# Reordering the front of a fused attention and mixer kernel: k casts, zero products, first pair and gathered rows, one relu

## The chip, the cores and the metric

The kernel runs on one core of a Trainium2 chip. The core has five engines, each with its own in-order instruction queue: TensorE (PE in the profile, with its weight loads PEld), VectorE (DVE), ScalarE (ACT), GpSimd (POOL) and SyncE (SP, which issues DMAs here). They meet only through semaphores. The metric is the time of one launch on the device, in microseconds (us); lower is better.

## The reference

Attention over 8 batches, 8 heads, 576 positions and 64 dimensions, in which a row sees its neighbours within 32 positions, and 8 global positions see all and are seen by all. What it gives is turned into `[batch, 576, 512]` and goes through a mixer: one two-layer product over positions, one over channels, each with a residual.

```python
scores = q @ k^T / 8;  mask = |i - j| <= 32 or global[i] or global[j]
x  = softmax(where(mask, scores, -1e9)) @ v            # heads side by side: [B, 576, 512]
u  = x + (relu(x^T @ w_tok1) @ w_tok2)^T               # 576 -> 256 -> 576
out = u + relu(u @ w_ch1) @ w_ch2                      # 512 -> 1536 -> 512
```

Inputs and output are float32; the kernel computes its products in float16 with float32 sums.

## The kernel before

Heads go in four pairs (`p`), rows in five tiles of 128 (`t`, `tau`), of which the last holds 64. For one batch the steps are:

- **casts** (`cast_qk`, L364, and L361 for the last 64 rows): q and k from float32 (`lq`, `lk`, `lr`) to float16 (`qk`, `rn`). q, k and v of batch 0 come in by DMAs on SP at the start; those of batch 1 by SP as well, once the casts have freed the buffers.
- **transposes**: `T` (L432) turns the four q and four k tiles of a pair on TensorE into a PSUM tile `pT`; `TE_q` and `TE_k` (L436, L442) copy it out in row order into `qT` and `kT`. `TR` (L454 to L456) does so for the last rows. From batch 3 on DMA transposes and the copies `order_k`, `order_q` take their place.
- **scores** (`S_`, L467): a band of scores per pair in two PSUM tiles, then exponentials on ScalarE (L487, L504, L509) into `e_all`. In batch 0 the mask is added on TensorE, as products of `far` with the identity (L475); `far` is built by `masks_r` and `masks_l` on VectorE out of `pcol`, five column products (L299). From batch 1 on `SM` multiplies the exponentials by `bandm` on VectorE (L531) and copies the global columns to `eg` (L525); in batch 0 it only copies (L521).
- **global rows**: `gather` (L205, four indirect DMAs on GpSimd for each half of the batches) fetches the q and k rows of the global positions by row numbers (`idx_i`, made in `row_numbers`); `gather_t` casts them on VectorE (L337), transposes them on TensorE (L338, tile `pg`) and copies them to `gT` and `kgz`. Batch 0 gets its own by products with a one-hot matrix (`G0`, L416). `GK` makes their scores, `OG` (L553) their part of the output, `PV` (L574 to L591) the weighted sum of v and the division.
- **mixer over positions**: `M1` (L606), a relu, `M2` (L630, L636, L639; for batch 0 also `M23_first` and `M3_first`, L647 to L663), giving `u`, and its transpose `uT` (by DMA from batch 1 on).
- **mixer over channels**: `M4`, twelve products `b1p` of four matmuls (L683) with a relu each: on ScalarE (L689), for odd ones of batch 0 on VectorE (L687); `M4l` for the last rows of two batches; `M5` (L712), `op`, in halves of six matmuls, with the residual added on VectorE (L716) and a store on SP.

The order is written out by hand; no scheduler moves anything, and each engine takes its instructions in the order of the program. The front of batch 0 stands at the end of the function. Then `period(b)` runs for each batch: it lists the channel products of batch `b` in `dense` (twelve M4, then M5 in halves), and `d(k)` takes the next `k` of them between the attention steps of batch `n = b + 1`. `scores(p, k)` is the attention step of one pair, `keep` holds some dense steps back for later, and `tail` says how many go early. PSUM has three double-bank buffers (`psS`, by `pss`) for scores, transposes, `pg`, `pv`, `hp` and `pcol`, and two single banks (`psM`, by `psm`) for `b1p` and `op`; `misc` and `idle` hold the latter two at first. A tile that takes a buffer waits for the last reader of the one before. Six products of zeros (L866) into `idle` stand at the very front; nothing reads them.

Of the kernel before, what the change touches and what calls it, by code (L numbers as in the profile page):

```python
# [26 lines left out]
def kernel(  # L27
# [32 lines left out]
    def pss(shape, dtype=F32, name="s"):  # L60
        return psS.tile(shape, dtype, tag="s", name=name)
# [211 lines left out]

    misc = psm([P, 512], name="misc")
    idle = psm([P, 512], name="idle")
    pcol = pss([P, 2, 512], name="pcol").rearrange("p a b -> p (a b)")

    def masks_0():
        gidx_h = const.tile([1, NG], F16)
# [15 lines left out]
        return isgb  # L295

    def column_products(isgb):
        for t in range(NT):
            nc.tensor.matmul(pcol[:, P * t : P * t + P], lhsT=isgb[:, t, :], rhs=ident, start=True, stop=True)  # L299

# [9 lines left out]

    def masks_r(c):
        nc.vector.scalar_tensor_tensor(
            out=far[:, c, 80:208], in0=pcol[:, P * c : P * c + P], scalar=rowok[:, c : c + 1], in1=right, op0=ALU.add,
            op1=ALU.add,
        )

    def masks_l(c):
        nc.vector.scalar_tensor_tensor(
            out=far[:, c, 0:64], in0=pcol[:, P * c - 64 : P * c], scalar=rowok[:, c : c + 1], in1=left, op0=ALU.add,
            op1=ALU.add,  # L320
        )

# [4 lines left out]
    def masks_c():  # L327
# [2 lines left out]
        nc.gpsimd.tensor_copy(out=it_f, in_=it_i)  # L330
        nc.gpsimd.tensor_scalar(out=mf, in0=it_f, scalar1=gpm, scalar2=hi8, op0=ALU.is_equal, op1=ALU.add)

    def gather_t(t):
        copy = nc.vector.tensor_copy
        pg = pss([P, 2, P], F16, name=f"pg_{t}")
        for ti in range(2):
            copy(out=g16[ti][t], in_=g32[ti][t])  # L337
            nc.tensor.transpose(out=pg[:, ti, :], in_=g16[ti][t], identity=ident)  # L338
        b0 = 1 if t == 0 else 0
        bs = slice(4 * t + b0, 4 * t + 4)  # L340
        pk = pg.rearrange("p i (b n g) -> p i b n g", b=4, n=NP)[:, :, b0:]
        copy(out=gT[:, bs], in_=pk[:, 0])
        for par in range(2):
            r = slice(64 * par, 64 * par + 64)
            copy(out=kgz[r, bs, :, GW * par + NG : GW * par + GW], in_=pk[r, 1])
# [50 lines left out]
    def order(b, p):  # L396
        order_k(b, p)
        order_q(b, p)
# [42 lines left out]
    def TE_k(b, p, copy):  # L441
        copy(  # L442
            out=kTs[b % 2][:, p, WIN : WIN + 512].rearrange("p (x i) -> p x i", i=4),
            in_=st[b]["pT", p][:, 1].rearrange("p (i x) -> p x i", i=4),
        )

    def TE(b, p, copy):
        TE_q(b, p, copy)
        TE_k(b, p, copy)

    def TR(b, copy):
        pr = pss([P, NP, P], F16, name=f"pr_{b}")
        for p in range(NP):
            nc.tensor.transpose(out=pr[:, p], in_=rn[:, p], identity=ident)  # L454
        copy(out=qTs[b % 2][:, :, NT - 1, GW : GW + LAST], in_=pr[:, :, 0:LAST])
        copy(out=kTs[b % 2][:, :, WIN + 512 : WIN + S], in_=pr[:, :, LAST:P])  # L456
# [208 lines left out]
    def M3(b, part):  # L665
# [7 lines left out]
        else:  # L673
            s["uTl"] = mb.tile([P, 4, P], F16, tag="uTl", name=f"uTl_{b}")
            nc.sync.dma_start_transpose(out=s["uTl"], in_=s["ul"])

    def M4(b, j):
        s = st[b]
        if j == 0:
            s["b1"] = mb.tile([P, NJ, 512], F16, tag="b1", bufs=1, name=f"b1_{b}")  # L680
        ps = psm([P, 512], name=f"b1p_{b}_{j}")
        for cc in range(4):
            nc.tensor.matmul(  # L683
                ps, lhsT=wc1[:, cc, P * j : P * j + P], rhs=s["uT"][:, cc, :], start=(cc == 0), stop=(cc == 3)
            )
        if b == 0 and j % 2:
            nc.vector.tensor_scalar(out=s["b1"][:, j, :], in0=ps, scalar1=0.0, scalar2=None, op0=ALU.max)  # L687
        else:
            nc.scalar.activation(out=s["b1"][:, j, :], in_=ps, func=AF.Relu)  # L689
# [35 lines left out]
    def d(k, keep=0):  # L725
        for _ in range(k):
            if len(dense) > keep:
                dense.pop(0)()
# [12 lines left out]
    def period(b):  # L741
        n, m = b + 1, b + 2
        odd = b % 2
        dense.extend(lambda j=j: M4(b, j) for j in range(NJ))
        if odd:
            dense.extend(lambda j=j: M4l(b, j) for j in range(3))
        dense.extend(lambda t=t, i=i: M5(b, t, i) for t in range(4 + odd) for i in range(2))
        if n == B:
            d(len(dense))
            return  # L750
        tail = len(dense) - (23 if odd else 20) - 2 * odd
        keep = 4 if n == 1 else 0

        def scores(p, k):

            es = S_all(n, p)
            es[0]()
            es[1]()
            d(1)
            es[2]()  # L760
            if n < 3 and p < 2:
                T(n, p + 2)
            d(1 + k)
            if n > 2 and p < 2:
                order(n, p + 2)
            SM(n, p)
            if n < 3 and p < 2:
                TE(n, p + 2, nc.vector.tensor_copy)

        if n == 1:  # L770
            d(2)
            gather_t(0)
            globals_(1)
            TR(1, act)
            T(1, 0)
            TE_q(1, 0, act)
            TE_k(1, 0, dve)
            d(1)
            T(1, 1)
            TE_q(1, 1, act)  # L780
            TE_k(1, 1, dve)
        if n > 2:
            load(n + 2)
        scores(0, tail > 5)
        scores(1, max(tail - 4 - (tail > 5), 0))
        scores(2, 0)
        GK(n)
        if n > 2 and m < B:
            turns(m)
        if n == 2:  # L790
            for c in casts(3, nc.gpsimd.tensor_copy):
                c()
            load(4)
            turns(3)
        d(1)
        scores(3, 0)
        if n == 1:
            c2 = casts(2, nc.scalar.copy)
            for c in c2[0:1] + c2[1::2]:
                c()  # L800
            load_v16(2)
            for p in range(NP):
                cast_qk(2, 1, p, nc.gpsimd.tensor_copy)
            load(3)
            gather(1)
        d(n > 1)
        OG(n)
        d(1)
        if n == 3:
            gather_t(1)  # L810
        fill = [order_rest, lambda i: order_k(i, 0), lambda i: order_q(i, 0), lambda i: order_k(i, 1), lambda i: order_q(i, 1)]
        for tau in range(NT):
            PV(n, tau)
            if 0 < tau < 4:
                M1(n, tau - 1)
            if n > 2 and m < B:
                fill[tau](m)
            if n == 2 and tau > 2:
                fill[tau - 3](m)
            if tau < 4 and n > 1:  # L820
                d(1)
        if m < B:
            globals_(m)
        M1(n, 3)
        if n == 2:
            order_q(3, 0)
        d(0 if n == 1 else len(dense) - (8 + 2 * odd), keep)
        M1(n, 4)
        d(1, keep)
        if 2 < m < B:  # L830
            load_v16(m)
        M2(n, 0)
        M3(n, 0)
        M2(n, 1)
        M3(n, 1)
        M2(n, 2)
        if n % 2:
            M3(n, 2)
        if 1 < n < B - 2:
            for c in casts(n + 2, nc.scalar.copy):  # L840
                c()
        if n == 1:
            TR(2, nc.scalar.copy)
            T(2, 0)
            TE(2, 0, nc.scalar.copy)
            d(1, keep)
            T(2, 1)
            TE(2, 1, nc.scalar.copy)
            d(1, keep)
        else:  # L850
            d(1)
            if n == 2:
                order(3, 1)
            d(1)

    act, dve = nc.scalar.copy, nc.vector.tensor_copy
# [5 lines left out]
    def cast0(ti, p, eng):  # L862
        cast_qk(0, ti, p, eng)

    for _ in range(6):
        nc.tensor.matmul(idle, lhsT=wz[:, 0:P], rhs=wz, start=True, stop=True)  # L866
    qk_pads(0)
    masks_0()
    masks_a1()
    cast0(0, 0, act)  # L870
    cast0(1, 0, act)
    isgb = masks_a2()
    T(0, 0)
    column_products(isgb)
    positions()
    masks_c()
    masks_a3()
    TE_k(0, 0, act)
    cast0(0, None, act)
    cast0(0, 1, act)  # L880
    TE_q(0, 0, dve)
    masks_r(1)
    masks_l(1)
    masks_r(2)
    masks_l(2)
    G0(0)
    cast0(1, 1, dve)
    exps(S_(0, 0, 0))
    masks_r(0)
    masks_r(NT - 1)  # L890
# [2 lines left out]
    masks_l(3)  # L893
    w_pads()
    pads(0)
    TR(0, dve)
    T(0, 1)
    TE(0, 1, dve)
    exps(S_(0, 0, 1))
    cast0(0, 2, act)  # L900
    G0(1)
    cast0(1, 2, dve)
    exps(S_(0, 1, 0))
    T(0, 2)
    cast0(0, 3, dve)
    TE(0, 2, dve)
    exps(S_(0, 1, 1))
    G0(2)
    cast0(1, 3, dve)
    T(0, 3)  # L910
    SM(0, 0)
    exps(S_all(0, 2))
    TE(0, 3, dve)
    G0(3)
    SM(0, 1)
    blocks()
    row_numbers()
    exps(S_all(0, 3))
    SM(0, 2)
    e_pads()  # L920
    castv(0, (0,))
    load_w1()
    castv(0, (1, 2, 3))
# [5 lines left out]
    gather(0)  # L929
    load_wc1(4)  # L930
    load_wc1(8)
    SM(0, 3)
    GK(0)
    OG(0)
    PV(0, 0)
# [22 lines left out]
    M3_first(1)  # L958
    M23_first(3)
    M3_first(2)  # L960
    M3_first(3)
    for c in c1[5::2]:
        c()
# [34 lines left out]
```

## Time and profile before

| | us |
|---|---|
| median of three runs | 323.25 (323.15 to 323.35) |
| profiled execution, time | 322.88 |
| profiled execution, span | 320.5 |
| TensorE busy | 302.5 (94%) |
| VectorE busy | 189.3 (59%) |
| ScalarE busy | 164.3 (51%) |
| GpSimd busy | 81.9 (26%) |

The span runs from the first to the last instruction of the program; the launch's time has some 2.4 us more around it. A timeline row gives start, duration, engine, line and operation, out<-in, count and, in brackets, how long the engine sat idle before and what ended that. Matmuls overlap: of a group the start is exact and the end modelled. A waits row gives who waited for whom, the total, how often and the longest, in us.

### The profile page before, as it was taken

To read this page: it belongs to the slowest core of one execution; us is meant where nothing else is said; L and a number is where in the kernel's file an instruction comes from. 1 tells how busy PE (TensorE), PEld (TensorE's weight loads), DVE (VectorE), ACT (ScalarE), POOL (GpSimd) and SP (SyncE) were. 2 spreads that over 40 slices of the span, in tenths; PEclk is the share of its full clock that TensorE was granted. 3 is DMA by queue.
4 is the path that set the end of the run, shared out by engine and by line. 5 is a ranking of instruction groups with operands and counts; after the bars stand their busy time and mean duration, and the time that the engine had idled before them with its cause. 6 is when DMAs were issued, how large, how long until landed. Compare 5 with 4: busy or idle time off the path is not lost.

```text
span 320.5 us, 6499 instructions
## 1 busy us (share of the span) xinstructions
PE 302.5 (94%) x2582; PEld 157.3 (49%) x2582; DVE 189.3 (59%) x412; ACT 164.3 (51%) x291; POOL 81.9 (26%) x131
## 2 busy tenths in 40 slices
PE   6879889889999999999999999999999999999994
PEld 2546353545366443644466445544565445544641
DVE  7777478754763667765873476757674565350021
ACT  5471678335745738284937557385733464305500
POOL 8966984763932000400041001400000000000000
PEclk9997999999999999999999999999999999999999
DMA  7999999998799999965997499945431620042022
GB/s 206 253 246 250 164 178 301 116 321 133 211 181 137 134 308 248 122 68 116 344 165 78 117 314 178 131 74 161 84 55 24 143 65 2 2 117 96 2 80 83
DMA packets 106751, 48.16 MB, mean 150 GB/s; under 512 B 86050, under 2 KB 100258, under 8 KB 106722
## 3 DMA queue, kind: packets, MB, share of 16 engines
q1 hardware_dynamic: 67600, 32.52, 45.7%
q0 software_dynamic: 39120, 15.24, 39.3%
q8 instruction: 20, 0.33, 0.5%
q14 instruction: 9, 0.07, 0.1%
q10 hardware_dynamic: 2, 0.00, 0.0%
HBM read 36.11 MB, written 9.44 MB: 142 GB/s over the span
## 4 chain that ended last, share of the span: by engine, by line
PE 80%; DVE 10%; ACT 6%; DMA 1%; issue 1%; SPq 1%; DVEq 0%; ACTq 0%
PE op L712 30%; PE b1p L683 21%; PE a1p L606 5%; PE s L467 4%; PE hp L630 4%; PE b1lp L699 3%; PE pv L574 3%; PE pv L583 3%; PE pv L579 2%; ACT e_all L487 2%; DVE x L591 2%; DVE e_all L531 1%; DMA lr<-in_k_dram 1%; ACT e_all L504 1%; PE pT L432 1%
## 5 line engine op out<-in xcount | busy, mean ns | idle before, releaser
L683 PE MATMUL b1p<-uT,wc 128*128 128x512 f16 x384 | 94.8, 380 | 1.5 <-DVE b L687 0.5
L712 PE MATMUL op<-wc,b 128*128 128x512 f16 x384 | 88.1, 379 | 0.0
L689 ACT ACTIVATE b<-b1p 128x512 f16<-128x512 f32 x90 | 54.4, 604 | 62.6 <-PE b1p L683 62.5
L712 PEld LDWEIGHTS <-b 128*128 128x128 f16 x384 | 36.3, 98 | 42.9
L683 PEld LDWEIGHTS <-wc 128*128 128x128 f16 x384 | 35.0, 98 | 44.3 <-issue 6.0
L353 POOL DMA_DIRECT2D vsh<-in_v_dram x35 | 30.0, 871 | 103.0 <-PE pv L583 97.4
L716 DVE TENSOR_TENSOR osb<-u,op 128x512 f32<-128x512 f16 x32 | 22.0, 687 | 52.3 <-PE op L712 52.2
L487 ACT ACTIVATE e_all<-s 128x832 f16<-128x832 f32 x32 | 27.6, 863 | 42.6 <-issue 31.7
L531 DVE TENSOR_TENSOR e_all<-e_all,bandm 128x1040 f16<-128x1040 f16 x56 | 36.7, 696 | 1.0
L636 DVE TENSOR_TENSOR u<-x,hp 128x512 f16<-128x512 f16 x28 | 17.4, 682 | 22.3 <-PE hp L630 22.3
L591 DVE TENSOR_TENSOR x<-pv,rr 128x512 f16<-128x512 f32 (+1 forms) x40 | 27.6, 691 | 1.4
L574 PEld LDWEIGHTS <-e_all 128*128 128x128 f16 x320 | 21.7, 99 | 5.4 <-issue 0.2
L574 PE MATMUL pv<-vsh,e_all 128*128 128x66 f16 x320 | 23.9, 196 | 0.0
L504 ACT ACTIVATE e_all<-s 128x576 f16<-128x576 f32 x32 | 20.7, 648 | 4.6 <-PE s L467 4.6
L579 PE MATMUL pv<-vsh,e_all 128*128 128x66 f16 x256 | 20.6, 196 | 0.0
L467 PE MATMUL s<-qT,kT 64*128 64x208 f16 (+1 forms) x320 | 19.6, 247 | 0.2 <-DVE kT L442 0.2
L606 PE MATMUL a1p<-x,w 128*128 128x512 f16 x64 | 19.0, 379 | 0.4 <-DVE x L591 0.3
L579 PEld LDWEIGHTS <-e_all 128*128 128x128 f16 x256 | 17.5, 100 | 3.3
L590 DVE RECIPROCAL rr<-pv 128x8 f32<-128x8 f32 (+1 forms) x40 | 8.2, 206 | 18.1 <-PE pv L583 17.8
L467 PEld LDWEIGHTS <-kT 64*128 64x128 f16 x320 | 11.3, 95 | 14.9 <-issue 11.0
L509 ACT ACTIVATE e_all<-s 128x416 f16<-128x416 f32 x32 | 17.0, 530 | 0.0
L630 PE MATMUL hp<-a,w 128*128 128x512 f16 x72 | 16.8, 378 | 0.0
(177 smaller groups left out, 349.4 us busy)
## 6 DMA issues: line engine op xcount, KB each, us to landing
out_dram<-osb SPq DMA_DIRECT2D x32, 256.0 KB, 2.3
lq<-in_q_dram SPq DMA_DIRECT2D x4, 1024.0 KB, 7.0
lk<-in_k_dram SPq DMA_DIRECT2D x4, 1024.0 KB, 9.4
wc<-in_moe_w_ch_dram POOLq DMA_DIRECT2D x6, 512.0 KB, 8.8
lq<-in_q_dram POOLq DMA_DIRECT2D x3, 1024.0 KB, 8.8
lk<-in_k_dram POOLq DMA_DIRECT2D x3, 1024.0 KB, 11.0
vsh<-in_v_dram POOLq DMA_DIRECT2D x21, 128.0 KB, 9.1
vsh<-in_v_dram POOLq DMA_DIRECT2D x14, 96.0 KB, 8.8
```

The lines of the kernel that those rows point to most:

```text
L353: nc.gpsimd.dma_start(out=vsh[b % 2][r0:r1, c, :, 0:D], in_=v[b, :, j0 : j0 + (r1 - r0), :].rearrange("h p d -> p h d"),)
L467: nc.tensor.matmul(ps[:, par, off : off + n], lhsT=kT[r, P * c : P * c + P], rhs=qf[r, lo : lo + n], start=b > 0, stop=b > 0 or c > 1 and ...
L487: nc.scalar.activation(out=e2[:, :, 1:3, 64:EW], in_=ps[:, :, 0 : 2 * W].rearrange("p h (c x) -> p h c x", c=2), func=AF.Exp, scale=scale,)
L531: nc.vector.tensor_mul(out=eh, in0=eh, in1=bandm)
L574: nc.tensor.matmul(o, lhsT=e_all[:, h, tau, EW - P - sh : EW - sh], rhs=vsh[b % 2][:, tau, h, :], start=hh == 0, stop=False,)
L579: nc.tensor.matmul(o, lhsT=e_all[:, h, tau + 1, 0:P], rhs=vsh[b % 2][:, tau + 1, h, :], start=False, stop=False)
L591: nc.vector.tensor_tensor(out=x16s[b % 2][r, tau, :].rearrange("p (f h x) -> p f h x", f=2, h=NP), in0=pq[r, :, :, 0:D], in1=rr[r].unsquee ...
L606: nc.tensor.matmul(ps[tt], lhsT=w, rhs=x16s[b % 2][:, ch, :], start=(ch == 0), stop=(ch == NT - 1))
L630: nc.tensor.matmul(ps[:, i, :], lhsT=w2[:, ch, P * tau - sh : P * tau - sh + P], rhs=s["a1"][:, ch, :], start=(ch == 0), stop=(ch == 1),)
L683: nc.tensor.matmul(ps, lhsT=wc1[:, cc, P * j : P * j + P], rhs=s["uT"][:, cc, :], start=(cc == 0), stop=(cc == 3))
L689: nc.scalar.activation(out=s["b1"][:, j, :], in_=ps, func=AF.Relu)
L712: nc.tensor.matmul(ps, lhsT=w, rhs=wc2[:, j, :], start=(j == 0), stop=(j == NJ - 1))
```

## The change

It moves and adds instructions; what is computed stays the same.

- In the front, the k casts of pairs 1 and 2 go from VectorE to ScalarE, both casts of pair 3 stay on VectorE and come earlier. Two and four more products of zeros follow the index product and the column products. `pcol` is allocated behind the first transposes. Pair 1 is transposed ahead of the last rows, the transposes of pair 2 go ahead of the scores of pair 1, and the row numbers and the first `eg` copies change places.
- The float32 to float16 casts of the gathered rows become `gather_c`, which stands ahead of the last `uT` copy of batch 0 (first half) and at the end of batch 2's period (second half).
- In the first period, the gathered rows, the last rows and pair 0 of batch 1 stand ahead of the channel products, one product more stands between the scores of pair 3 and `OG`, one output half comes after the third `PV`, and the transposes of batch 2 follow one output half instead of being spread between two. `keep` is 3 instead of 4.
- While the scores of pair 3 are made in batches 3 to 7, the relu of one `b1p` (j = 3 of the batch before) goes to VectorE.

```diff
-    pcol = pss([P, 2, 512], name="pcol").rearrange("p a b -> p (a b)")
+    pc = {}
...
     def column_products(isgb):
+        pc["col"] = pcol = pss([P, 2, 512], name="pcol").rearrange("p a b -> p (a b)")
...
+    def gather_c(t):
+        for ti in range(2):
+            nc.vector.tensor_copy(out=g16[ti][t], in_=g32[ti][t])
+
     def gather_t(t):
         copy = nc.vector.tensor_copy
         pg = pss([P, 2, P], F16, name=f"pg_{t}")
         for ti in range(2):
-            copy(out=g16[ti][t], in_=g32[ti][t])
             nc.tensor.transpose(out=pg[:, ti, :], in_=g16[ti][t], identity=ident)
...
-        if b == 0 and j % 2:
+        if b == 0 and j % 2 or relu_on_dve[0]:
             nc.vector.tensor_scalar(out=s["b1"][:, j, :], in0=ps, scalar1=0.0, scalar2=None, op0=ALU.max)
...
-        keep = 4 if n == 1 else 0
+        keep = 3 if n == 1 else 0
...
             es[1]()
+            relu_on_dve[0] = n > 2 and p == 3
             d(1)
+            relu_on_dve[0] = False
             es[2]()
...
         if n == 1:
-            d(2)
             gather_t(0)
...
             TE_k(1, 1, dve)
+            d(1)
...
-        d(n > 1)
+        d(1)
         OG(n)
...
-            if tau < 4 and n > 1:
+            if tau < 4 and n > 1 or tau == 2:
                 d(1)
...
         if n == 1:
-            TR(2, nc.scalar.copy)
+            d(1, keep)
+            TR(2, act)
             T(2, 0)
-            TE(2, 0, nc.scalar.copy)
-            d(1, keep)
+            TE(2, 0, act)
             T(2, 1)
-            TE(2, 1, nc.scalar.copy)
-            d(1, keep)
+            TE(2, 1, act)
         else:
             d(1)
             if n == 2:
                 order(3, 1)
+                gather_c(1)
...
-    for _ in range(6):
-        nc.tensor.matmul(idle, lhsT=wz[:, 0:P], rhs=wz, start=True, stop=True)
+    def fill(k):
+        for _ in range(k):
+            nc.tensor.matmul(idle, lhsT=wz[:, 0:P], rhs=wz, start=True, stop=True)
+
+    fill(6)
     qk_pads(0)
     masks_0()
+    fill(2)
...
     column_products(isgb)
+    fill(4)
...
     cast0(0, 1, act)
+    cast0(1, 1, act)
...
     G0(0)
-    cast0(1, 1, dve)
     exps(S_(0, 0, 0))
...
     pads(0)
+    cast0(0, 2, act)
+    cast0(1, 2, act)
+    T(0, 1)
     TR(0, dve)
-    T(0, 1)
     TE(0, 1, dve)
     exps(S_(0, 0, 1))
-    cast0(0, 2, act)
     G0(1)
-    cast0(1, 2, dve)
-    exps(S_(0, 1, 0))
+    cast0(0, 3, dve)
+    cast0(1, 3, dve)
     T(0, 2)
-    cast0(0, 3, dve)
+    exps(S_all(0, 1))
     TE(0, 2, dve)
-    exps(S_(0, 1, 1))
     G0(2)
-    cast0(1, 3, dve)
     T(0, 3)
-    SM(0, 0)
     exps(S_all(0, 2))
     TE(0, 3, dve)
     G0(3)
+    row_numbers()
+    exps(S_all(0, 3))
+    SM(0, 0)
     SM(0, 1)
     blocks()
-    row_numbers()
-    exps(S_all(0, 3))
     SM(0, 2)
     e_pads()
+    SM(0, 3)
...
-    SM(0, 3)
     GK(0)
...
     M3_first(2)
+    gather_c(0)
     M3_first(3)
```

More of the change, by code (lines that the diff above doesn't have):

```diff
@@ L312, in masks_r @@
         nc.vector.scalar_tensor_tensor(
-            out=far[:, c, 80:208], in0=pcol[:, P * c : P * c + P], scalar=rowok[:, c : c + 1], in1=right, op0=ALU.add,
+            out=far[:, c, 80:208], in0=pc["col"][:, P * c : P * c + P], scalar=rowok[:, c : c + 1], in1=right, op0=ALU.add,
             op1=ALU.add,
@@ L318, in masks_l @@
         nc.vector.scalar_tensor_tensor(
-            out=far[:, c, 0:64], in0=pcol[:, P * c - 64 : P * c], scalar=rowok[:, c : c + 1], in1=left, op0=ALU.add,
+            out=far[:, c, 0:64], in0=pc["col"][:, P * c - 64 : P * c], scalar=rowok[:, c : c + 1], in1=left, op0=ALU.add,
             op1=ALU.add,
@@ L675, in M3 @@
             nc.sync.dma_start_transpose(out=s["uTl"], in_=s["ul"])
+    relu_on_dve = [False]
     def M4(b, j):
```

## The prediction

> **What bounds the kernel now.** I read the page first, then busy time by stage, then TensorE's waits by stage, then the timeline wherever a wait was long.
>
> ```profile
> span 320.5 us, 6499 instructions
> ```
>
> ```profile
> 0.00:24.30 24.30, 18.16 (x175) 9.88 (x175) 18.74 (x72) 14.05 (x23) 19.54 (x47) 1.00 0.93 235
> ...
> 37.70:58.00 20.30, 17.53 (x158) 8.76 (x159) 15.76 (x32) 15.23 (x30) 12.45 (x18) 1.00 1.48 222
> ...
> 73.70:300.00 226.30, 224.90 (x1868) 114.85 (x1868) 133.90 (x268) 123.11 (x218) 27.08 (x33) 1.00 0.82 134
> ```
>
> Columns: stretch, length, then busy time of PE, PEld, DVE, ACT and POOL with their instructions. From 73.7 us on TensorE is busy 224.9 of 226.3 us: only gaps within its own groups can be won there. It waits in the front (to 24.3) and in the first period (37.7 to 73.7); the token mixing of batch 0 between them is not edited. The waits, one row from 0:24.3, four from 37.7:58, two from 58:72:
>
> ```profile
> PE og L553 <- DVE eg L521: 1.7, 1, 1.7
> ...
> PE pg L338 <- DVE g_k L337: 1.3, 1, 1.3
> PE og L553 <- DVE eg L525: 0.8, 1, 0.8
> PE b1p L683 <- DVE b L687: 0.5, 1, 0.5
> PE s L467 <- DVE kT L442: 0.2, 1, 0.2
> ...
> PE pT L432 <- ACT kT L456: 0.7, 1, 0.7
> PE a1p L606 <- DVE x L591: 0.7, 2, 0.4
> ```
>
> Since TensorE is full behind 73.7 us, time won ahead of it reaches the end, unless a load comes too late for it.
>
> **Part 1, the front** (k casts of pairs 1 and 2 to ScalarE, six zero products, pair order). Timeline rows:
>
> ```profile
> 1.20 2.74 PE L866 MATMUL idle<-wz 128*128 128x512 f16 x6 [1.20 <-DVE wz L114]
> 6.72 2.52 POOL L331 TENSOR_SCALAR mf<-it_f,gpm,hi 128x640 f16<-128x640 f32 x1
> 8.57 2.06 DVE L364 CAST qk<-lk 128x512 f16<-128x512 f32 x1
> 9.55 0.86 ACT L487 ACTIVATE e_all<-s 128x832 f16<-128x832 f32 x1 [1.07 <-PE s L467]
> 12.70 0.68 DVE L442 COPY kT<-pT 128x512 f16<-128x512 f16 x1
> 13.39 0.65 ACT L504 ACTIVATE e_all<-s 128x576 f16<-128x576 f32 x1 [2.97 <-PE s L467]
> 13.57 0.85 PE L475 MATMUL s<-far,ident 128*128 128x416 f16 x2
> 13.87 0.42 DVE L364 CAST qk<-lk 128x512 f16<-128x512 f32 x1
> 14.33 0.62 ACT L364 CAST qk<-lq 128x512 f16<-128x512 f32 x1
> 15.01 1.04 PE L432 MATMUL pT<-ident,qk 128*128 128x128 f16 x8
> 18.61 0.52 PE L475 MATMUL s<-far,ident 128*128 128x416 f16 x2
> 19.45 0.86 ACT L487 ACTIVATE e_all<-s 128x832 f16<-128x832 f32 x1 [0.96 <-PE s L467]
> 24.09 0.15 DVE L521 COPY eg<-e_all 128x160 f16<-128x160 f16 x1
> ```
>
> ```profile
> 14.00:17.40 3.40, 3.28 (x28) 1.92 (x27) 1.91 (x4) 1.79 (x4) 3.35 (x6) 1.00 0.87 185
> 18.35 0.37 SPq L86 DMA_DIRECT2D lk<-in_k_dram  x1
> ```
>
> Two things are bought. First, the k cast of pair 1 took VectorE 2.06 us where the same cast took 0.42 later; GpSimd's operation of 2.52 us was running when the slow one began. With it and the cast of 13.87 VectorE loses 2.48 us of work; ScalarE takes 2 x 0.62 = 1.24 us more, inside the 2.97 us that it idled ahead of 13.39. Second, the clock: the same two mask products took 0.85 us at 13.57 and 0.52 at 18.61, so TensorE ran at half rate at first, and at full rate only behind the stretch from 14 to 17.4 us, of which it was busy 3.28 of 3.40. In the changed order the queue holds, from the index product on, 2 zero products, 8 transposes, 5 column products and 4 zero products. At half rate a zero product takes about 0.43 us (six in 2.74, less the last one's tail) and a transpose or column product about a quarter, 0.11: 6 x 0.43 + 13 x 0.11 = 4.0 us without a hole, then the scores of pair 0. The rise should come between 7 and 10 us.
>
> I replayed the new order by hand with these durations and each queue in order. At full clock from about 7 us: first exponentials at 9.2 (now 9.55), kT of pair 1 done 11.9 (now 13.38), exponentials of pair 2 from 15.0 (now 19.45), last eg copy at 19.8 (now 24.09): 4.3 us won. At half clock to 17.4 us: 9.65, 12.8, 18.2, 23.0: 1.1 us won. I take 3.6, near the upper end because the unbroken stretch is there, less 0.7 because the VectorE casts of pair 3 now come at about 12.1, when GpSimd starts on the v casts, so that one of them may be held as the cast at 8.57 was. What is late next is VectorE itself (copies, clears, eg). The clears of e_all stay between the same two eg copies: zero. Two queues move with this. On SP the k load of batch 1, held to 18.35 by the last k cast, is issued some 3 us earlier, right behind the q load; it shares the DMA engines with weights that are not needed before 28 us, so I price it at nothing (rival 2 if that is wrong). On GpSimd the four gathers, and the channel weights behind them, wait for the row numbers, which now come ahead of two eg copies: some 2 us earlier.
>
> The Trainium skill, "TensorE: Matmul & The Clock Gate", Part 4, says that transposes do not count as activity for the clock gate as products do. By that the 8 transposes of pair 0 would be a hole, and the sum would hold 1.1 in place of 3.6. The trace speaks against it: the rise at about 17.4 us followed a stretch that held the 1.04 us of transposes.
>
> **Part 2, batch 1's first pair and gathered rows ahead of the channel products** (37.4 to 73.7 us).
>
> ```profile
> 31.26 2.29 POOL L364 CAST qk<-lk 128x512 f16<-128x512 f32 x4 [2.28 <-DMA lk<-in_k_dram]
> 37.61 0.68 DVE L639 TENSOR_TENSOR ul<-x,hp 64x512 f16<-64x512 f16 x1
> 71.24 0.59 ACT L442 COPY kT<-pT 128x512 f16<-128x512 f16 x1
> L531 DVE TENSOR_TENSOR e_all<-e_all,bandm 128x1040 f16<-128x1040 f16 x56 | 36.7, 696 | 1.0
> ```
>
> Removed from the listed waits (4.2 us): the 1.3 for the gathered rows (their casts now fill VectorE's gap ahead of the last uT copy), the 0.8 at og (one more channel product stands ahead, and the relu of b_11 goes behind eg), the 0.7 at pT (an output half now stands there, op_1b), and about 1.1 of the 1.4 at b1p, kT and a1p (op_0b now follows pv_2; its eviction joins VectorE's x copies, under TensorE's longer work): 3.9. New waits: pT of pair 0 takes the buffer that ul is read from until 38.29, while TensorE comes, by the replay, at about 37.9: 0.4. The scores of pair 2 wait for kT: behind the relu of b_3 VectorE has eg, two mask products of 0.70 and two copies of about 0.6, some 3.4 us with the relu, against some 2.8 of TensorE's: 0.6. The scores of batch 2, pair 0, follow the two transposes directly, while ScalarE still has four copies of up to 0.59: 1.0. Net 3.9 - 2.0 = 1.9. Bounds: 3.9 if the new waits are covered; 1.9 - 1.6 = 0.3 if the casts of the gathered rows (at about 32 now) meet GpSimd's four k casts, by the 1.6 that the cast at 8.57 lost.
>
> **Part 3, steady state** (relu of b_3 to VectorE from batch 2 on, while the scores of batch 3 and later are made; casts of the second gathered rows earlier).
>
> ```profile
> 123.14 3.06 PE L683 MATMUL b1p<-uT,wc 128*128 128x512 f16 x12
> ...
> 127.97 0.23 PE L338 MATMUL pg<-ident,g_q 128*128 128x128 f16 x1 [0.39 <-DVE g_q L337]
> ...
> 147.84 4.06 PE L712 MATMUL op<-wc,b 128*128 128x512 f16 x18
> ...
> 156.02 3.06 PE L683 MATMUL b1p<-uT,wc 128*128 128x512 f16 x12
> ...
> 157.40 0.62 ACT L689 ACTIVATE b<-b1p 128x512 f16<-128x512 f32 x1
> 158.46 0.24 DVE L525 TENSOR_TENSOR eg<-e_all,bandm 128x160 f16<-128x160 f16 x1 [1.42 <-ACT e_all L509]
> ...
> 262.91 3.06 PE L683 MATMUL b1p<-uT,wc 128*128 128x512 f16 x12
> ```
>
> Eighteen products took 4.06 us; by that twelve take about 4.06 - 6 x 0.217 = 2.76, but took 3.06: b1p_5 waits 0.30 for its buffer, which ScalarE's relu of b_3, behind two exponentials, frees late. It stands so in the five batches from 123.14 to 262.91. VectorE idles 1.42 us just then, so its relu starts when the product ends: about 0.25 x 5 = 1.25, and eg comes no later, since the last exponential moves up by the 0.62. With 0.4 for pg: 1.7. Bounds 0 (VectorE comes late from lf) and 1.9.
>
> **Sum.** The profiled execution took 322.88 us, 2.4 around its span and 0.37 below the median of 323.25. 3.6 + 1.9 + 1.7 = 7.2: 315.7 against the profiled one, 316.0 against the median, which is my forecast. By the Part 4 sentence it would be 318.5.
>
> **Rivals.**
>
> ```profile
> 35.79 4.25 POOL L353 DMA_DIRECT2D vsh<-in_v_dram x5
> ```
>
> ```profile
> 26.40 0.95 POOL L205 DMA_INDIRECT g_k<-in_k_dram,idx_i  x1 [0.32 <-issue]
> ```
>
> ```profile
> DMA to landing us min/median/max: 6.4/7.0/7.7
> ```
>
> 1. The zero products do not raise the clock early (it asks for a longer stretch, or transposes count as pause): part 1 gives 1.1, 318.5 us. For: the first six, 2.74 us, did not raise it. Against: 4.0 us without a hole.
> 2. Loads take the front's gain back. GpSimd's k casts already waited 2.28 us for a landing, and the v loads, issued behind them up to 40.04, do not come earlier. The first product on them would start at about 51; if they land later, part 1 is lost: 323.25 - 1.9 - 1.7 = 319.7. Against: gathers, 7.7 us at most to landing, suggest 48.
> 3. Slower: TensorE and VectorE now stand in order behind the gathered rows at about 32 us, with nothing ahead to cover. The last gather, issued at 26.40 now, landed by about 35 at the latest; it will be issued some 2 us earlier. Each us beyond 32 costs one; above 32 + 7.2 + 0.7 = 39.9 the change is slower, and a landing at 41 gives 325. That is nearly twice the slowest landing seen.
>
> **How the numbers follow.** Forecast 0.64, its own range 313.8 to 317.6 (parts 1 and 2 at their better ends; a held cast in each). Rival 1 0.17, rival 2 0.10, rival 3 0.05; 0.04 for no change that can be told, which is within 0.2%, 0.65 us, about what this kernel's measurement can tell. Faster 0.91, same 0.04, slower 0.05. The range, 313.6 to 319.7, takes in rivals 1 and 2.
>
> **What would show it.** Part 1: no VectorE cast of 2 us, mask products at 0.5 us before 11 us, og before 21.5. Part 2: pg directly behind hp, s of batch 1 at about 37, no wait at og. Part 3: b1p groups of twelve at 2.8, no wait at pg. I am wrong if mask products still take 0.85 at 13 us, if uT's last copy waits for g_k, or if og of batch 1 waits for a DMA.

## The result, and the profile after

The changed kernel's runs took 317.50 to 319.52 us, median 318.19; the kernel before, beside it on the same chip, 323.2. The ratio is 0.985 (0.981 to 0.989): 4.8 us won, with an interval from 3.5 to 6.0. The forecast was 316.0, so 2.2 us too much was expected, inside the range given. The profiled execution took 317.50 us. Ratios, here and below, leave out an execution that ran over 1.5% above the fastest one of its kernel; that was one, with plain loads.

First the page's span and busy time by stage of the changed kernel, columns as before:

```profile
span 315.7 us, 6514 instructions
```

```profile
0.00:24.30 24.30, 19.29 (x244) 11.44 (x245) 18.82 (x73) 15.28 (x25) 19.95 (x48) 0.94 0.90 230
24.30:37.70 13.40, 10.60 (x92) 5.66 (x90) 8.99 (x21) 6.68 (x13) 8.35 (x15) 0.98 1.09 208
37.70:58.00 20.30, 19.28 (x202) 10.01 (x200) 16.32 (x31) 14.38 (x26) 13.79 (x20) 1.00 1.40 226
...
73.70:300.00 226.30, 225.21 (x1894) 116.48 (x1891) 137.81 (x272) 121.78 (x214) 29.92 (x36) 1.00 0.84 135
```

TensorE is still full behind 73.7 us. What was won has to be followed by where each stage starts. The table holds the starts of TensorE's first instruction of a stage in the two timelines, and how far the changed kernel is ahead there (from unrounded times):

| stage | before, us | after, us | ahead |
|---|---|---|---|
| `gk` of batch 0 | 22.05 | 17.78 | 4.27 |
| `pv` of batch 0 | 24.95 | 20.95 | 4.00 |
| `hp` of batch 0 | 32.90 | 31.02 | 1.88 |
| scores of batch 2, pair 0 | 73.69 | 69.48 | 4.21 |
| first `b1p` of batch 1 | 81.47 | 78.71 | 2.76 |
| `og` of batch 2 | 88.74 | 85.73 | 3.02 |
| end of the span | 320.5 | 315.7 | 4.8 |

So the front gave 4.27 us, as much as the replay's better end; 2.4 of them were gone thirteen microseconds later, between `gk` and `hp` of batch 0, most of them (2.1) behind the start of `pv`. The first period added 1.14 (1.88 to 3.02), the steady state 1.77 (3.02 to 4.79).

Rows of the changed kernel's timeline, from the front to `hp`:

```profile
6.07 1.03 PE L875 MATMUL idle<-wz 128*128 128x512 f16 x4
...
8.16 0.51 PE L479 MATMUL s<-far,ident 128*128 128x416 f16 x2 [0.46 <-DVE far L319]
...
15.19 0.86 ACT L491 ACTIVATE e_all<-s 128x832 f16<-128x832 f32 x1 [0.38 <-PE s L471]
...
20.26 0.23 DVE L525 COPY eg<-e_all 128x160 f16<-128x160 f16 x1
...
21.42 1.07 POOL L205 DMA_INDIRECT g_q<-in_q_dram,idx_i  x1 [0.31 <-issue]
...
23.10 0.63 PE L587 MATMUL pv<-rf,lf 128*128 128x264 f16 x2
...
24.97 0.21 DVE L594 RECIPROCAL rr<-pv 128x8 f32<-128x8 f32 x1 [1.58 <-PE pv L578]
...
27.31 0.21 DVE L594 RECIPROCAL rr<-pv 128x8 f32<-128x8 f32 x1 [0.78 <-PE pv L587]
...
31.02 1.12 PE L651 MATMUL hp<-a,w 128*128 128x512 f16 x4 [0.47 <-ACT a L615]
```

The four zero products take 1.03 us, 0.22 apart: full rate at 6.07 us. The mask products at 8.16 take 0.51, the exponentials of pair 2 come at 15.19 (forecast 15.0) and the last `eg` copy at 20.26 (19.8). Then the odd thing: the second `pv` is complete by its row at 23.10 + 0.63 = 23.73, and its reciprocal, with VectorE idle, starts at 24.97. In the timeline of the kernel before the same reciprocal came 0.04 us behind the product's end, 27.77:

```profile
27.14 0.63 PE L583 MATMUL pv<-rf,lf 128*128 128x264 f16 x2
...
27.81 0.21 DVE L590 RECIPROCAL rr<-pv 128x8 f32<-128x8 f32 x1 [0.38 <-PE pv L583]
```

The third reciprocal comes late too, and `a1p` and `hp` behind them.

TensorE's waits of the changed kernel, one row from 22 to 37.7 us, one from 37.7 to 58, three from 37.7 to 74, one from 73 to 300:

```profile
PE pT L436 <- DVE ul L643: 0.3, 1, 0.3
...
PE s L471 <- DVE kT L446: 0.7, 1, 0.7
...
PE a1p L610 <- DVE x L595: 0.7, 2, 0.4
...
PE s L471 <- ACT kT L446: 0.6, 1, 0.6
PE pT L436 <- ACT kT L446: 0.3, 1, 0.3
...
PE s L471 <- DVE kT L446: 0.9, 1, 0.9
```

The waits for gathered rows and at `og` are gone; the two at `a1p`, 0.7 us, are as before. The new ones that were forecast are there (rows one, two, four and five), and one at 78.2 us (the last row) that was not.

### The profile page after: what moved, and what is told of

Read it like the earlier page. It is cut to its first block, busy times and chain, and to the rows that moved or that the text cites. A ratio compares the mean times of both kernels' runs of the same rounds, so it can differ in the third digit from the quotient of the medians.

```text
span 315.7 us, 6514 instructions
## 1 busy us (share of the span) xinstructions
PE 299.6 (95%) x2588; PEld 155.9 (49%) x2588; DVE 192.7 (61%) x415; ACT 163.6 (52%) x288; POOL 82.5 (26%) x131
## 4 chain that ended last, share of the span: by engine, by line
PE 74%; DVE 2%; ACT 1%; issue 0%
PE op L718 27%; PE b1p L689 23%; PE hp L634 4%; PE a1p L610 4%; PE b1lp L705 3%; PE s L471 3%; PE pv L578 2%; PE pv L587 2%; PE pv L583 2%; PE og L557 1%; DVE e_all L535 1%; PE gk L544 1%; ACT b L695 0%; PE gk L545 0%; ACT e_all L491 0%; DVE osb L725 0%
## 5 line engine op out<-in xcount | busy, mean ns | idle before, releaser
L695 ACT ACTIVATE b<-b1p 128x512 f16<-128x512 f32 x85 | 51.1, 601 | 61.2 <-PE b1p L689 61.0
L535 DVE TENSOR_TENSOR e_all<-e_all,bandm 128x1040 f16<-128x1040 f16 x56 | 37.4, 709 | 1.0
L471 PE MATMUL s<-qT,kT 64*128 64x208 f16 (+1 forms) x320 | 18.8, 241 | 2.3 <-DVE kT L446 1.6
L368 ACT CAST qk<-lq 128x512 f16<-128x512 f32 x27 | 16.2, 618 | 6.7 <-DMA lq<-in_q_dram 6.2
## 6 DMA issues: line engine op xcount, KB each, us to landing
vsh<-in_v_dram POOLq DMA_DIRECT2D x14, 96.0 KB, 10.1
```

The costliest lines, as they stand in the source:

```text
L471: nc.tensor.matmul(ps[:, par, off : off + n], lhsT=kT[r, P * c : P * c + P], rhs=qf[r, lo : lo + n], start=b > 0, stop=b > 0 or c > 1 and ...
L535: nc.vector.tensor_mul(out=eh, in0=eh, in1=bandm)
```

## The experiments

Three groups of four kernels, each group on one chip together with the kernel before; intervals are those of the ratio to it. The groups ran on three chips.

### Part 1 alone, and parts 2 and 3 alone

```diff
-    for _ in range(6):
-        nc.tensor.matmul(idle, lhsT=wz[:, 0:P], rhs=wz, start=True, stop=True)
+    fill(6)
...
+    cast0(0, 2, act)
+    cast0(1, 2, act)
+    T(0, 1)
     TR(0, dve)
-    T(0, 1)
...
```

The front's hunks of the change on the kernel before:

> The kernel before with part 1 alone. If the front's gain went through as forecast, 3.6 us: about 319.6. If most of what is won by the scores of the last pair (4.27 us in the changed kernel) is always lost again while the first batch's weighted sums of v and a1p are made (1.88 left at hp), about 321.3, and the shift at hp is again near 1.9 us. If that loss was an accident of the one execution that was profiled, the shift at hp is above 3 us.

```diff
-        keep = 4 if n == 1 else 0
+        keep = 3 if n == 1 else 0
...
+            relu_on_dve[0] = n > 2 and p == 3
             d(1)
...
+    gather_c(0)
     M3_first(3)
```

All the other hunks on the kernel before:

> Parts 2 and 3 without part 1: the front is that of before. By the forecast's terms 1.9 + 1.7 = 3.6 us: 319.6. If what part 2 lost against its forecast (1.1 in place of 1.9) comes from the order alone, 1.1 + 1.8 = 2.9: 320.3. If it comes from the stages standing some 3 us earlier against GpSimd's casts, the masks of batch 2's first pair take VectorE 1.3 us again, not 2.0, and the time is 319.6 or below.

Part 1 alone: 321.40 us, ratio 0.993 (0.991 to 0.995), 2.2 us won of the 3.6 forecast. Parts 2 and 3: 320.25 us, 0.990 (0.987 to 0.994), 3.1 us won of 3.6. The sum, 5.3, is what the whole change gave in this group (5.4, next). In the trace of part 1 alone `gk` starts at 17.36 and `hp` at 30.81: 4.7 us ahead of before, then 2.1. The loss between them is no accident of one execution.

The second trace held a surprise: its front is that of before, line for line, yet the k cast of pair 1 took 0.43 us there, not 2.06, and `gk` started at 20.29, not 22.05. The masks of batch 2's first pair took 1.31 us, as before, and the wait at 78.2 us was absent; instead the first scores of batch 2 waited 2.0 us, not 0.6, for ScalarE's copies. That execution was the slowest of its four (322.07 us).

### The same kernels again, and zero products where TensorE waits

> The changed kernel unchanged, for what repeats. If the loss between og and hp is a property of the order, hp starts again at about 31.0 us and the rows of reciprocals stand at 22.5, 25.0 and 27.3 us. If it is chance (one code fetch that came late), hp starts up to 1 us earlier or later while the rows to 18 us stay within 0.1 us. Time 317.5 to 319.5 in both.

```diff
     GK(0)
+    fill(8)
     OG(0)
```

> The changed kernel with eight more products of zeros (1.7 us at full clock) between gk and og of batch 0, where TensorE waits 1.8 us for the last eg. If the half clock that is granted from 21.5 to 24.9 us follows from that wait and costs the front's gain, the clock stays at 1.00 there, a1p starts 0.5 us or more earlier and the time falls by 0.5 to 1.0 us. If late code or late loads set the pace from og to hp, the clock stays up and hp starts within 0.3 us of before.

The changed kernel again: 318.26 us, 0.983 (0.981 to 0.986). With the eight zero products: 318.63, 0.985 (0.981 to 0.988), no difference that can be told. Busy time by stage, first of the changed kernel, then with the zero products (the third column from the right is the granted clock):

```profile
21.00:23.00 2.00, 1.79 (x34) 1.56 (x34) 1.22 (x3) 0.45 (x1) 1.39 (x3) 0.62 0.97 299
23.00:25.00 2.00, 2.00 (x27) 1.70 (x25) 0.41 (x2) 0.57 (x2) 1.70 (x2) 0.53 1.16 279
```

```profile
21.00:23.00 2.00, 1.57 (x41) 1.41 (x38) 0.71 (x1) 0.00 (x0) 1.64 (x2) 1.00 1.18 307
23.00:25.00 2.00, 0.97 (x17) 0.63 (x13) 0.87 (x2) 1.14 (x2) 1.45 (x2) 1.00 1.15 247
```

The half clock came behind the wait for `eg`, and the zero products took it away, but `hp` did not move: 31.46 us here and 31.46 in the changed kernel run again. VectorE's reciprocals, again first, then with the zero products:

```profile
24.05 0.21 DVE L594 RECIPROCAL rr<-pv 128x8 f32<-128x8 f32 x1 [2.28 <-PE pv L587]
26.37 0.21 DVE L594 RECIPROCAL rr<-pv 128x8 f32<-128x8 f32 x1 [1.38 <-PE pv L587]
```

```profile
24.09 0.21 DVE L594 RECIPROCAL rr<-pv 128x8 f32<-128x8 f32 x1 [2.30 <-PE pv L587]
26.37 0.21 DVE L594 RECIPROCAL rr<-pv 128x8 f32<-128x8 f32 x1 [1.35 <-PE pv L587]
```

The same times to 0.04 us, though TensorE ran at half and at full clock. So neither TensorE's pace nor VectorE's sets them. What stands equal in the two is GpSimd: its first gather starts at 20.51 us in both. That made the gathers the suspect. In all eight traces in which VectorE is late in this way, the last late reciprocal starts 5.7 to 5.9 us behind the first gather, though that gather starts anywhere from 19.77 to 21.66 us; `hp` follows 5.9 to 6.0 us later where it is the first reciprocal, 5.1 to 5.2 where the second, 3.7 where the third.

The traces also record when a semaphore is updated, and there the lateness shows itself. In the changed kernel run again, a `pv` product ends by its row at 23.75 us; TensorE's update comes at 26.35, and VectorE starts at 26.37. So VectorE is not what is held. Away from the gathers every product's update comes within 0.06 us of its row's end.

### The kernel before a second time

> The kernel before, unchanged, for a second trace of it. The sum was made against one execution, in which one k cast took 2.06 us and TensorE ran at half rate to 17.4 us; with the same front, the kernel with parts 2 and 3 alone had the cast at 0.43 us, full rate from 12.5 us and gk 1.76 us earlier. If that execution of before was an unlucky one, gk starts at 20.3 to 21.5 us here, not at 22.05, and part 1 was forecast too high by as much; if it is the rule for this order, gk stands at 22.0 again.

The median is 323.55 us, ratio 1.001 (0.998 to 1.005). `gk` starts at 21.25, 0.8 us earlier than in the trace that the sum was made against, and `hp` at 33.33, 0.4 later: here, too, VectorE waited 1.5 us for a reciprocal. The trace of before that the forecast rests on was late in the front and short from `gk` to `hp` (10.85 us; 12.08 here).

### Plain loads for the gathers

```diff
     def gather(t):
         for ti in range(2):
             for par in range(2):
+                if t == 0:
+                    nc.gpsimd.dma_start(out=g32[ti][t][:, par, :], in_=rows[ti][P * par : P * par + P])
+                    continue
```

On the changed kernel:

> The changed kernel in which the first four gathers are replaced by plain loads of as many fixed rows on the same queue, so the global rows of batches 1 to 3 are wrong; nothing else differs. If it is the gathers that hold TensorE's signals to VectorE back by up to 3 us while the first batch's weighted sums are made, no reciprocal of batch 0 waits over 1 us, hp starts 1 us or more earlier than at 31.0 to 31.5 us, and up to 1 us of it reaches the end. If code fetches or the load traffic hold them, hp starts at 31.0 to 31.5 us again and the time is 317.5 to 319.1.

On the kernel before:

> The kernel before with its first four gathers replaced by plain loads of as many fixed rows (the global rows of batches 1 to 3 are then wrong), to weigh the change where no gather holds TensorE's signals. Against the changed kernel with the same replacement (315.3 to 316.7 us): if the forecast's terms hold apart from the gathers, the difference is about 7 us and this runs at 322 to 323; if the gathers cost both kernels the same, it runs at 320.5 to 321.5, and the difference is about 5.

On the changed kernel the median is 316.72 us; the ratio, 0.976 (0.969 to 0.983), is of the three executions of 315.24 to 318.01. `gk` starts at 17.33, `hp` at 27.76, and the reciprocals of its timeline no longer wait:

```profile
21.83 0.21 DVE L597 RECIPROCAL rr<-pv 128x8 f32<-128x8 f32 x1 [0.48 <-PE pv L590]
22.68 0.20 DVE L597 RECIPROCAL rr<-pv 128x8 f32<-128x8 f32 x1
24.06 0.20 DVE L597 RECIPROCAL rr<-pv 128x8 f32<-128x8 f32 x1
```

That is 3.3 to 3.7 us earlier at `hp` than with gathers. About 1.0 us of it is the clock: the granted clock stayed at 1.00 here behind the same wait of 1.72 us at `og`, and a trace below with `gk` at 17.33, no late signal and the half clock has `hp` at 28.73. The interval of the ratio overlaps that of the changed kernel on the other chips, so a gain in the time is not shown.

The same trace holds its own comparison. Around the plain loads (19.98 to 22.16 us) no update of TensorE is late. Its second four gathers, left as they were, start at 64.78 us, and there the updates are late again, the last at 70.63, 5.85 us behind the first of them. Seven of the eight late traces have late updates around the second gathers too; that is where the 2.0 us wait of parts 2 and 3 alone comes from, whose copies on ScalarE waited for them.

The profiled execution was the slowest of the four (320.64 us): it stood 6.6 us ahead of before when the scores of batch 2, pair 1, were made, and then lost five in one wait of TensorE for the DMA transposes of `u`. How much the other three lost there can't be told:

```profile
PE b1p L692 <- DMA uT<-u: 5.1, 1, 5.1
```

On the kernel before, in the third group, plain loads changed nothing: 322.49, ratio 1.000 (0.997 to 1.002). Taken together, 7.9 us (5.6 to 10.1) of change without the gathers and 7.2 forecast agree; but the two kernels ran on different chips, and the next runs show that this matters.

### The gathers moved

```diff
             load(3)
-            gather(1)
...
             load_v16(m)
+        if n == 2:
+            gather(1)
...
+        if n == 3:
+            gather_c(1)
         GK(n)
...
                 order(3, 1)
-                gather_c(1)
```

> The changed kernel with the second four gathers (rows of batches 4 to 7, first used at about 125 us) moved from 64 to 69 us to about 98 us, behind the v loads of batch 3, and their casts to the period that uses them. If the gathers hold TensorE's signals in the transposes of batch 2 too, no transpose at 68 us is copied late, ScalarE's copies of the second pair follow those of the first without the 0.9 to 1.2 us pause, and the time falls by 0.3 to 1.0 us. If the adjacent transposes alone make the wait, the pause and the time stay.

```diff
-    gather(0)
     load_wc1(4)
     load_wc1(8)
+    gather(0)
```

> The changed kernel with two of the channel weight loads ahead of the first four gathers on GpSimd, so that these start at about 22.5 in place of 20.5 to 21.4 us. If they hold TensorE's signals for up to 2.3 us at a time, from about 0.7 to 2.8 and 3.5 to 5.8 us behind their start, the first two reciprocals come on time (22 to 24 us), and hp starts 0.5 to 1.5 us earlier than at 31.0 to 31.5; the gathered rows land some 1.5 us later and may take part of it back, so 0 to 1 us less in all. If the hold does not move with the gathers, hp does not move.

> Both moves together. If they add: 0.5 to 1.5 us below the changed kernel, 316.7 to 317.7; if the transposes of u by DMA, which end at about 74 to 80 us, set the pace of batch 1's channel stage by then, no more than the better one of the two.

Second gathers late: 315.98 us, ratio 0.984 (0.979 to 0.988), no more than the change itself had won on the other chips. First gathers behind the weights: 320.34, 0.994 (0.992 to 0.997); both: 321.37, 0.998 (0.995 to 1.000). With the second gathers late, the wait of 0.6 us at batch 2's first scores stayed, so it does not come from them. No signal was late in any of the four traces of this group, not even with the gathers where they had stood. The reciprocals with the second gathers moved, and with the first gather at 20.51 us as above:

```profile
22.30 0.21 DVE L594 RECIPROCAL rr<-pv 128x8 f32<-128x8 f32 x1 [0.73 <-PE pv L587]
23.62 0.21 DVE L594 RECIPROCAL rr<-pv 128x8 f32<-128x8 f32 x1 [0.39 <-PE pv L587]
```

`hp` starts at 28.73 there, 4.16 us ahead of before, the scores of batch 2 stand 6.5 ahead, and the span is 313.5. So gathers alone do not hold the signals. VectorE's reads of `og` or `pv` are late in eight traces, all with gathers in this place: seven of the first two groups and that of the changed kernel. The one trace of those groups without gathers there, with plain loads, is on time in this place and late at its second gathers; all four on the third chip are on time, two of them with gathers moved by at most 1.3 us and one with the first ones unmoved, and so was the first trace of before. The gathers are needed for the hold, as far as these runs go, and something else besides, which stays open. The changed kernel itself was not run on the third chip, so what the second gathers cost in the time stays open too.

The second move shows rival 3 at work. The rows queue behind the weights on GpSimd's DMA queue and land late, and VectorE stands before their cast (its timeline, first gathers behind the weights):

```profile
36.78 0.79 DVE L336 CAST g_q<-g_q 128x128 f16<-128x128 f32 x1 [4.44 <-DMA g_q<-in_q_dram,idx_i]
```

TensorE waits 3.6 us behind it, and the 3.6 us by which `hp` was early (29.32) are gone.

### One half of part 1 undone each

```diff
     masks_0()
-    fill(2)
...
     column_products(isgb)
-    fill(4)
```

> The changed kernel without its six added products of zeros. If they bring the full clock forward, the first mask products take 0.67 to 0.85 us in place of 0.51, gk starts 0.5 to 2 us later than at 17.3 to 17.8 us, and the time rises by up to 1 us. If the clock comes early without them, gk stands within 0.2 us and the time is the changed kernel's.

```diff
-    cast0(1, 1, act)
...
     G0(0)
+    cast0(1, 1, dve)
...
-    cast0(1, 2, act)
...
     G0(1)
+    cast0(1, 2, dve)
```

> The changed kernel with the k casts of pairs 1 and 2 back on VectorE, where they stood before. By the forecast VectorE loses 0.43 + 0.42 us where nothing slows it, 2.5 where GpSimd's operation meets the first: gk starts 0.4 to 2.5 us later than at 17.3 to 17.8, and og with it. If hp is set by what holds TensorE's signals, hp moves by less than half of that and the time by under 0.7 us.

Without the added zero products: 319.45 us, 0.989 (0.981 to 0.996); the first mask products and the transposes of pair 2 in its timeline:

```profile
8.19 0.85 PE L479 MATMUL s<-far,ident 128*128 128x416 f16 x2 [0.73 <-DVE far L319]
...
12.47 1.01 PE L436 MATMUL pT<-ident,qk 128*128 128x128 f16 x8
```

Half rate to 12.5 us and beyond, `gk` at 19.29: the added zero products bring 1.5 to 2.0 us there, against 17.78 and 17.33 in the two traces of the changed kernel. This repeats: in all nine traces with the added products the first mask products take 0.51 us, in the five without them 0.67 to 0.85. By the clock records full rate begins between 4.35 and 7.21 us in the nine and lasts past 20 us. In the five it begins at 13.76 to 17.39 us in three; in two (before a second time, parts 2 and 3 alone) it begins at 4.68 and 5.01 and is lost again 3.41 us later. So the added products do two things: they bring full rate early in every trace, and they hold it. With the casts back on VectorE: 318.65, 0.984 (0.979 to 0.990); the casts took 0.41 and 0.42 us, and `gk` starts at 18.66, 0.9 to 1.3 later. At `hp` both differences have shrunk: 31.65 and 30.73 stand against 31.02 and 31.46. In the time neither can be told from the changed kernel.

## Why the prediction was right, and where it was too high

The time fell inside the range by some luck. The forecast's own range, 313.8 to 317.6, misses the measured 318.19; the wider one holds it because it takes in rivals 1 and 2, and neither of these came about. The time stands 0.3 us from rival 1's 318.5, which the rows refute. (The lower end of the own range does not follow from its bounds either: 316.0 less 0.7 and 2.0 is 313.3.)

**Part 1** (3.6 forecast, 2.2 measured) failed in one sentence: that time won ahead of the full stretch reaches the end unless a load comes too late. Its own mechanism held. No VectorE cast of 2 us is left, the mask products take 0.51 us before 11 us, the rest of `og` runs from 20.55 (forecast: before 21.5), and 4.27 us were won at `gk`. Rival 1 is refuted: full rate stood at 6.07 us, and is not there at 8.19 without the added products. What took 2.4 us back was none of the rivals' loads but the stretch from `gk` to `hp`, taken as of fixed length: it took 10.85 us in the trace of before, and 13.24 in that of after. Late signals of TensorE to VectorE, seen only around gathers of GpSimd, stretch it: they are held to 5.7 to 5.9 us behind the first gather, and the gathers came forward by 1.0 us (22.46 to 21.42), `gk` by 4.27, so more of the held time became bare. On the third chip, with the same front and no late signal, the stretch takes 11.4 to 11.6 us. By that, an estimate across chips, 1.6 to 1.8 of the 2.4 us are the late signals, and 0.6 to 0.8 the changed order's own. No row of the trace of before showed late signals; the second trace of before does (12.08).

By the Trainium skill, "TensorE: Matmul & The Clock Gate", Part 4, transposes do not bring the full clock as products do. The traces speak against it here. In the timeline of parts 2 and 3 alone, without added zero products, the rate rose between two groups of transposes:

```profile
4.26 0.61 PE L435 MATMUL pT<-ident,qk 128*128 128x128 f16 x4 [0.21 <-POOL band L243]
5.14 0.40 PE L435 MATMUL pT<-ident,qk 128*128 128x128 f16 x4 [0.28 <-ACT qk L367]
```

These rows alone do not settle it, as six zero products ended only 0.3 us before them. The clock records add more. Every stretch at half clock in them, but the one at a span's end, lasts 3.41 us or twice that, so the clock seems to be set anew every 3.41 us. The 3.41 us ahead of the rise at 13.76 us in the kernel before with plain loads were busy for 3.31, of which 1.01 with transposes; in part 1 alone, one step ahead of its rise at 7.21 us, the 3.41 us to 3.80 us were busy for 2.60 with zero products, and no rise followed. Without the transposes the first would have had 2.30, less than the second.

The forecast also took two odd rows of one execution as the rule: the 2.06 us cast took 0.41 to 0.43 in all four other traces that have it on VectorE, and in three with the front of before `gk` came at 20.29, 20.93 and 21.25, not at 22.05. In the pair of profiled executions this cancelled against the late signals.

**Part 2** (1.9 forecast, 1.14 in the traces). Of the 3.9 us of waits that were to go, 3.5 went; the two at `a1p` (0.7 us), of which 0.4 had been counted as gone, stayed. Two waits of 0.2 that were not counted went too: 3.8. Of the forecast new ones, `pT` behind `ul` took 0.3 (0.4), the scores of pair 2 behind `kT` 0.7 (0.6), and batch 2's first scores and the transposes behind them 0.6 + 0.3 (1.0): 1.9 against 2.0. Not foreseen were the 0.9 us at 78.2 us. Their cause stands in the timeline of the changed kernel, with a cast of GpSimd that ran beside it:

```profile
74.94 2.01 DVE L535 TENSOR_TENSOR e_all<-e_all,bandm 128x1040 f16<-128x1040 f16 x2
...
75.33 1.08 POOL L368 CAST qk<-lq 128x512 f16<-128x512 f32 x1
```

Two mask products take VectorE 1.31 us otherwise and a cast takes GpSimd 0.61; here both are longer. GpSimd's casts of batch 3, which came spread out and missed the masks in the trace of before, now came in a row from 73.65 us, while VectorE's masks had moved 3.4 us earlier (78.31 to 74.94). In the trace of parts 2 and 3 alone no cast ran beside these masks, and they took 1.31. The list of new waits looked only at order on VectorE, not at what ran beside it. 3.8 less 2.8 is 1.0, near the 1.14 of the starts. The Trainium skill, "SBUF — State Buffer", section "SBUF: two separate sides", says that VectorE with two operands in SBUF and a GpSimd operation that reads SBUF lock each other out of a shared port; the rows agree in that both lengthen.

One sign of part 2 was missed together with the front's gain: the first scores of batch 1 came at 39.18 us, not at about 37. With no late signal, in the trace with the second gathers moved, they came at 36.89.

**Part 3** (1.7 forecast, 1.77 in the traces) was right in its sum and its mechanism; one of the groups of twelve in the changed kernel's timeline:

```profile
152.13 2.84 PE L689 MATMUL b1p<-uT,wc 128*128 128x512 f16 x12
```

2.84 in place of 3.06, and the starts move ahead by 0.87 us at the first such place with `pg`, and by 0.22 at each of the four that follow. So the five groups gave 1.1 (1.25 forecast) and `pg` 0.65 (0.4): two small misses that cancel.

So 3.6 + 1.9 + 1.7 became 1.88 + 1.14 + 1.77 = 4.79, the gain of the span.

## What to carry to other kernels

A gain in a latency-bound front is worth only what is left of it at the next stage with its own pace; compare the starts of the same instruction, stage by stage, and cost the stages between as if they could stretch. One trace is one execution: a row that looks odd (a cast of 2.06 us beside others of 0.42) should be priced at both values. When work on one engine moves, look at what then runs beside it on the other engines, not only at its own queue.

## What was not expected of the hardware

- VectorE waited up to 2.3 us for results of TensorE whose rows had ended, in eight traces and only around GpSimd's indirect DMAs; in two of them at the same times to 0.04 us, though TensorE's own pace differed. TensorE's semaphore updates come late there, and the last hold ends 5.6 to 5.9 us behind the first gather of the front. With plain loads in their place, and in every trace of one chip, they do not. Whether the products end later than their rows say or only the signal is late, the traces do not tell.
- A granted clock of 1.00 at the start of a profile says nothing: in the trace of before it reads 1.00 while the mask products take 0.85 us in place of 0.51, but the clock record begins only at 17.39 us. Where a record begins earlier, the half clock shows (the third number from the right), as in the second trace of before, whose mask products at 8.18 us take 0.85:

```profile
8.50:11.80 3.30, 2.88 (x23) 1.93 (x22) 2.02 (x9) 0.86 (x1) 3.13 (x8) 0.50 1.09 299
```

- The kernel before itself runs at medians of 323.7, 323.3 and 321.9 us on the three chips; on the last, no signal was late.
